# K^T U with 48 stationary columns instead of 64, and its sum into the state in two additions of 48 rows

## The chip, the core and the metric

The kernel runs on one core of a Trainium2 chip. The metric is the device time of one execution in microseconds. The engines of the core are named as in the profile: PE (TensorE, matmuls), PEld (TensorE's loads of the stationary operand, which overlap its matmuls), DVE (VectorE), ACT (ScalarE), POOL (GpSimd) and SP (SyncE, which issues most DMAs).

## What is computed

Two parts follow each other. The first is a delta-rule attention over 4 batches, 8 heads and 768 steps with heads of 48; its result, as 3072 tokens of 384, goes through a two-layer block with an exact GELU (384 to 2048 to 384). Everything is fp32.

```python
# attention: B, H, S, D = 4, 8, 768, 48; k_n is k over its norm
state = zeros(B, H, D, D)
for t in range(S):
    y[:, :, t] = einsum('bhd,bhde->bhe', q[:, :, t], state)
    v_old = einsum('bhde,bhd->bhe', state, k_n[:, :, t])
    state = state + beta_t * einsum('bhd,bhe->bhde', k_n[:, :, t], v_t - v_old)
# second part
x = y.transpose(0, 2, 1, 3).reshape(B * S, H * D)
out = gelu(x @ w_in) @ w_out          # moe_w_in 384 x 2048, moe_w_out 2048 x 384
```

## The kernel before

**Tiling.** The 768 steps are cut into NC = 12 chunks of C = 64 steps. The four batches form two units (a = 0, 1) of two batches each: batch p of a unit lies on partitions 64p to 64p + 63 (HALF[p]), one step per partition, the 8 heads beside each other. A chunk is worked out by matrices instead of step by step: Gram matrices of K (grams), a triangular inverse per head (eliminate_steps on DVE or POOL, then join and join_both through PE), the product of K and Q with the state (against_state, L731; against_queries, L751), the solved update rows U (solve, L791), the outputs (use, L821), and the new state, which is the old one plus K^T U (update, L832, and next_state, L837).

**The state** lies in SQ, a tile of 128 partitions. Its first 48 free elements per head pair are the state (the view St), the 64 after them the transposed Q of the unit. Heads with even number (r = 0) have their 48 state rows on partitions 0 to 47, those with odd number (r = 1) on partitions 64 to 111. Partitions 48 to 63 and 112 to 127 of St are set to zero at the start. Products that read the state or transposed K take rows r\*64 to r\*64 + 47 only.

**K** lies in Kp with 64 elements per head, of which the last 16 are set to zero once (L183) and stay so; the transposes of two heads at a time use that padding.

**K^T U.** For each unit and each chunk but the last, update() issues 16 matmuls: four head pairs j, and the four combinations (r, p) of QUADS. Stationary is K of one head and batch on 64 partitions, moving is U of the same (64 x 48). The result goes to PSUM on the partitions of half r. The PSUM tile psY of two banks holds the outputs (psY) and beside them this sum (psS). The matmuls of one batch and one r use one quarter of the array, so four quarters work side by side.

**After it**, outputs() runs on each unit in turn: next_state() adds psS into the state on DVE (L837), and read() makes the unit's output rows from psY with three DVE instructions (L847; from chunk 2 on): one over all 128 rows and two that swap the halves. When both units are read, turns() (L883; turn(), L873, for chunks 0 and 2) transposes the result on PE, ACT copies it to SBUF as xT, and the two-layer block takes it from there. In chunks 0 and 1 the reads are on ACT (L845), and chunk 0's additions stand after other work on DVE.

**The two-layer block** of chunks 0 and 1 is plain matmuls (fc1 L906, fc2 L924). From chunk 2 on it runs in a form with seven products of halves for eight, with sums made on DVE and ACT: part_of_layer (L1023) for the first layer, second_layer (L957) for the second, mix_x (L988) for sums of xT, mix (L1090 to L1095) for sums of the GELU's result. Its products are chained to each other in order by behind(). The weights arrive with 8 bytes per number and are decoded to fp32 by DVE and ACT up to about 111 us (begin, exponents, mantissas, signed: L251 to L281); each decoded part frees a slot, into which SP fetches the next (L233).

**What sets the order.** Up to chunk 0's additions, all engines run in the order in which the code is written. From there on, a plan gives each step a time in chunks, the steps are written out in the order of these times, and only DVE and POOL run in just that order (manual_schedule, L1429). The order on PE, ACT and SP is chosen by the framework's planner, which places ready instructions by its own estimate of durations, within the dependencies; `together` chains the matmuls of one step to those written before, and `behind` the products of the two-layer block. The waits between engines follow from what the instructions read and write.

Of the kernel before, what the change touches and what calls it, by code (L numbers as in the profile page):

```python
# [14 lines left out]
ALU = mybir.AluOpType  # L15
# [4 lines left out]
def kernel(  # L20
# [28 lines left out]
    nc = tc.nc  # L49
    B, H, S, D = q.shape  # L50
    DM, DF = moe_w_in.shape
    C = 64
# [8 lines left out]
    HALF = [slice(0, C), slice(C, 2 * C)]  # L61
# [10 lines left out]
    def dn(name):  # L72
        return ps.tile([128, 2, 512], F32, tag="dn", name=name)
# [29 lines left out]
    for c in range(NC):  # L103
        for a in range(NA):
            u = tiles[c, a] = Unit()
# [97 lines left out]
    St = SQ[:, :, :, :, 0:D]  # L203
# [602 lines left out]
    def use(us):  # L806

        for u in us:
            if u.c == 0 and u.a == 0:
                u.psY = [ps.tile([128, NP * D], F32, tag="mlp", name="psY").rearrange(  # L810
                    "q (k r d) -> q k r d", r=2, d=D) for s in range(2)]
            else:
                psY = dn("psY")
                both = quarters(psY[:, :, 0:NP * D])
                u.psY = [both[:, s] for s in range(2)]
                u.psS = psY[:, :, NP * D:2 * NP * D].rearrange("q p (j d) -> q p j d", d=D)
            for k in range(NP // 2):
                for r in range(2):
                    for p, s in SIDES:
                        h = 4 * k + 2 * s + r  # L820
                        nc.tensor.matmul(u.psY[s][HALF[p ^ s], k, r, :], lhsT=u.P[HALF[p], h, :],  # L821
                                         rhs=u.U[HALF[p], h, :], start=True, stop=True)
            if u.c > 0:
                update(u)

    def update(u):
        if u.c == 0 and u.a == 0:
            u.psS = dn("psS")[:, :, 0:NP * D].rearrange("q p (j d) -> q p j d", d=D)
        if u.c < NC - 1:
            for j in range(NP):  # L830
                for r, p in QUADS:
                    nc.tensor.matmul(u.psS[HALF[r], p ^ r, j, :], lhsT=u.Kp[HALF[p], 2 * j + r, :],  # L832
                                     rhs=u.U[HALF[p], 2 * j + r, :], start=True, stop=True)

    def next_state(u):
        if u.c < NC - 1:
            nc.vector.tensor_tensor(St[:, u.a], St[:, u.a], u.psS, op=ALU.add)  # L837

    def read(u, copy=nc.scalar.copy):
        u.x = u.U if u.c else wk.tile([128, H, D], F32, tag="y", name="x")  # L840
# [8 lines left out]
    def outputs(us):  # L849
        use(us)  # L850
        for u in us:
            next_state(u)
            read(u)
# [423 lines left out]
    mantissas(2)  # L1277
    turn(first[0])
    update(first[0])
    exponents(1)  # L1280
    turn(first[1])
    update(first[1])
    exponents(2)
    signed(1)
    for u in first[:NA]:
        next_state(u)
# [174 lines left out]
```

## Time and profile before

| | us |
|---|---|
| median of 3 runs | 629.37 (628.44 to 629.87) |
| the profiled execution | 629.47 |
| its span, first to last instruction | 627.7 |
| PE busy in L832, all records | 15.1 |
| DVE busy in L837, 22 instructions | 12.2 |
| mean granted TensorE clock | 0.986 of full speed |

The profile comes from one execution. Its page gives the busy time of each engine, and the busy share in 40 slices of the span (15.7 us each; a 9 is 90% or more). The chain of work that ended last is followed back from the last instruction, at each step to what released it. In the timeline and the groups, a row has the start and the duration in us, the engine, the line of the kernel, the operation, what it writes and reads, the shape and how many instructions are merged in it; in brackets the idle time of the engine before it and what ended that. A row of several merged instructions lasts from the first one's start to the last one's end. An fp32 matmul shows as two loads and two matmul records. Matmul ends are modelled.

The stage up to about 165 us holds the loading and decoding of the weights and chunks 0 to 2 of the attention; from there to 540 us chunks 3 to 11 and the two-layer block of the chunks before run side by side; the rest is the two-layer block of the last two chunks.

### The profile page before, as it was taken

To read this page: it belongs to the slowest core of one execution; us is meant where nothing else is said; L and a number is where in the kernel's file an instruction comes from. 1 tells how busy PE (TensorE), PEld (TensorE's weight loads), DVE (VectorE), ACT (ScalarE), POOL (GpSimd) and SP (SyncE) were. 2 spreads that over 40 slices of the span, in tenths; PEclk is the share of its full clock that TensorE was granted. 3 is DMA by queue.
4 is the path that set the end of the run, shared out by engine and by line. 5 is a ranking of instruction groups with operands and counts; after the bars stand their busy time and mean duration, and the time that the engine had idled before them with its cause. 6 is when DMAs were issued, how large, how long until landed. Compare 5 with 4: busy or idle time off the path is not lost.

```text
span 627.7 us, 19675 instructions
## 1 busy us (share of the span) xinstructions
PE 606.6 (97%) x8358; PEld 541.4 (86%) x8358; DVE 428.5 (68%) x793; ACT 240.6 (38%) x546; POOL 212.8 (34%) x316
## 2 busy tenths in 40 slices
PE   6779999999999999999999999999999999999997
PEld 4667886776899999998899998899998899988997
DVE  6999899999867598564859555859546946422432
ACT  3476876615443255224451134452134222044200
POOL 4045002000379821885222884223884200000000
PEclk9985999999999999999999999999999999999999
DMA  9695766001423452453123533013321001000011
GB/s 135 155 284 145 162 146 180 23 3 38 74 38 47 78 92 35 69 105 39 16 45 54 101 62 38 12 33 62 64 50 18 11 2 28 8 19 1 0 26 26
DMA packets 159575, 39.63 MB, mean 63 GB/s; under 512 B 151168, under 2 KB 154368, under 8 KB 159488
## 3 DMA queue, kind: packets, MB, share of 16 engines
q1 hardware_dynamic: 156816, 37.34, 30.9%
q10 hardware_dynamic: 2672, 1.03, 0.8%
q8 instruction: 66, 1.08, 0.7%
q14 instruction: 21, 0.17, 0.1%
HBM read 33.62 MB, written 4.72 MB: 61 GB/s over the span
## 4 chain that ended last, share of the span: by engine, by line
PE 81%; DVE 10%; DMA 4%; SPq 2%; issue 1%; ACT 1%; DVEq 0%
PE psX L957 13%; PE psY L1023 11%; PE psY L957 9%; PE psX L1023 8%; PE psV L1023 6%; PE psZ L1023 5%; PE psZ L957 4%; PE psV L957 4%; PE psK L731 3%; PE psO L924 3%; PE psG L439 2%; DMA w_raw<-in_moe_w_out_dram 2%; PE psH L906 2%; PE psY L821 2%; PE psU L791 2%; PE psQ L751 2%
## 5 line engine op out<-in xcount | busy, mean ns | idle before, releaser
L376 POOL TENSOR_TENSOR n<-n,half 128x16 f32<-128x16 f32 x10 | 30.9, 3091 | 176.1 <-DVE n L374 118.4
L529 POOL TENSOR_TENSOR Nu<-Nu,tmp 128x30 f32<-128x30 f32 (+14 forms) x120 | 65.7, 548 | 9.4
L527 POOL TENSOR_TENSOR tmp<-Nu 128x30 f32<-128x30 f32 (+14 forms) x120 | 62.5, 521 | 9.4
L1023 PE MATMUL psX<-xT,w_in_sb 128*128 128x256 f32 (+1 forms) x288 | 62.5, 346 | 0.0
L957 PE MATMUL psX<-w_out_sb,G 128*128 128x192 f32 x320 | 56.4, 329 | 0.0
L957 PEld LDWEIGHTS psX<-w_out_sb,G 128*128 128x128 f32 x320 | 52.1, 190 | 0.8
L1023 PEld LDWEIGHTS psX<-xT,w_in_sb 128*128 128x128 f32 x288 | 47.9, 191 | 5.3
L906 PE MATMUL psH<-xT,w_in_sb 128*128 128x256 f32 x192 | 45.8, 395 | 0.7 <-ACT G L912 0.5
L906 PEld LDWEIGHTS psH<-xT,w_in_sb 128*128 128x128 f32 x192 | 37.1, 197 | 8.0 <-ACT G L912 1.4
L924 PE MATMUL psO<-w_out_sb,G 128*128 128x384 f32 x128 | 43.9, 490 | 0.0
L1051 DVE TENSOR_TENSOR psY<-psY,pu 128x512 f32<-128x512 f32 x20 | 14.0, 700 | 40.9 <-PE psY L1023 40.3
L1023 PE MATMUL psY<-xT,w_in_sb 128*128 128x256 f32 (+1 forms) x192 | 41.5, 345 | 0.0
L1006 ACT COPY pu<-psZ 128x512 f32<-128x512 f32 x40 | 23.5, 587 | 38.7 <-PE psZ L1023 36.3
L1006 ACT COPY xT<-psX 128x768 f32<-128x768 f32 x9 | 7.2, 799 | 81.1 <-PE psX L883 81.1
L924 PEld LDWEIGHTS psO<-w_out_sb,G 128*128 128x128 f32 x128 | 23.5, 190 | 14.2 <-issue 0.3
L1023 PEld LDWEIGHTS psY<-xT,w_in_sb 128*128 128x128 f32 x192 | 32.1, 191 | 3.5
L837 DVE TENSOR_TENSOR SQ<-SQ,psY 128x384 f32<-128x384 f32 x21 | 11.6, 552 | 32.5 <-PE psY L832 32.2
L1006 ACT ACTIVATE G<-G 128x512 f32<-128x512 f32 x40 | 25.2, 631 | 19.8 <-DVE G L1059 19.6
L1006 ACT ACTIVATE G<-psY 128x512 f32<-128x512 f32 x20 | 11.9, 596 | 47.4 <-PE psY L1023 47.4
L1059 DVE TENSOR_TENSOR G<-psY,pu 128x512 f32<-128x512 f32 x20 | 13.8, 690 | 22.2 <-PE psY L1023 21.5
L957 PE MATMUL psY<-w_out_sb,G 128*128 128x192 f32 x160 | 28.1, 329 | 0.0
L957 PE MATMUL psZ<-T,pu 128*128 128x192 f32 x160 | 28.1, 329 | 0.0
(204 smaller groups left out, 1374.6 us busy)
## 6 DMA issues: line engine op xcount, KB each, us to landing
Kp<-in_k_dram SPq DMA_DIRECT2D x76, 96.0 KB, 3.2
w_out_sb<-in_moe_w_in_dram SPq DMA_DIRECT2D x24, 256.0 KB, 5.5
w_raw<-in_moe_w_out_dram SPq DMA_DIRECT2D x16, 384.0 KB, 5.2
V<-in_v_dram SPq DMA_DIRECT2D x48, 96.0 KB, 3.1
out_dram<-o_sb SPq DMA_DIRECT2D x40, 96.0 KB, 2.2
Qp<-in_k_dram SPq DMA_DIRECT2D x64, 32.0 KB, 2.3
Qp<-in_q_dram SPq DMA_DIRECT2D x96, 16.0 KB, 2.0
Qp<-in_k_dram SPq DMA_DIRECT2D x64, 16.0 KB, 2.1
```

Source lines behind the costliest of these rows:

```text
L376: nc.gpsimd.tensor_tensor(flat, flat, half, op=ALU.pow)
L439: nc.tensor.matmul(psG[HALF[p], r, i * NP + j, :], lhsT=u.Kt[rows, p, j, :], rhs=(u.Qt if x else u.Kt)[rows, p, j, :], start=True, stop=True)
L527: rows_on.tensor_tensor(tmp, nu[:, j + 1:, j:j + 1].to_broadcast([128, n, j]), nu[:, j:j + 1, 0:j].to_broadcast([128, n, j]), op=ALU.mult)
L529: rows_on.tensor_tensor(nu[:, j + 1:, 0:j], nu[:, j + 1:, 0:j], tmp, op=ALU.add)
L731: nc.tensor.matmul(u.psK[HALF[p], r, j, :], lhsT=u.Kt[rows, p, j, :], rhs=SQ[rows, u.a, p ^ r, j, 0:w], start=True, stop=True)
L906: nc.tensor.matmul(psH, lhsT=w_in_sb[:, f // 2, m, f % 2 * 128:(f % 2 + 1) * 128], rhs=xTs[c][:, m, :], start=(m == 0), stop=(m == NM - 1))
L924: nc.tensor.matmul(u.psO, lhsT=G[:, u.a, f, :], rhs=w_out_sb[:, f, :], start=(f == 0), stop=(f == NF - 1))
L957: nc.tensor.matmul(ps_, lhsT=lhs[:, f, :], rhs=rhs[:, f, :], start=first and f == 0, stop=f == FH - 1, skip_group_check=not first)
L1006: i = fn(*args, **kw)
L1023: nc.tensor.matmul(ps_[:, i], lhsT=lhs[:, f // 2, f % 2 * 128:(f % 2 + 1) * 128], rhs=rhs, start=first and i == 0, stop=True, skip_group_c ...
L1051: nc.vector.tensor_tensor(L1["Y1"], L1["Y1"], L1["pu"][:, 0], op=ALU.add)
L1059: nc.vector.tensor_tensor(half(1, 1), shaped(L1["Y1"]), shaped(L1["pu"][:, 0]), op=ALU.add)
```

## The change

The stationary operand of K^T U loses the 16 zero columns of Kp: 48 columns instead of 64. The result then covers 48 partitions of each half of PSUM instead of 64, and partitions 48 to 63 and 112 to 127 of psS are not written any more. next_state() adds the two pieces of 48 rows (partitions 0 to 47, and 64 to 111) in two DVE instructions instead of one over 128 partitions. The number of matmuls, their moving operand and all else stay as they are.

```diff
             for j in range(NP):
                 for r, p in QUADS:
-                    nc.tensor.matmul(u.psS[HALF[r], p ^ r, j, :], lhsT=u.Kp[HALF[p], 2 * j + r, :],
+                    nc.tensor.matmul(u.psS[r * C:r * C + D, p ^ r, j, :],
+                                     lhsT=u.Kp[HALF[p], 2 * j + r, 0:D],
                                      rhs=u.U[HALF[p], 2 * j + r, :], start=True, stop=True)
 
     def next_state(u):
         if u.c < NC - 1:
-            nc.vector.tensor_tensor(St[:, u.a], St[:, u.a], u.psS, op=ALU.add)
+            for r in range(2):
+                rows = slice(r * C, r * C + D)
+                nc.vector.tensor_tensor(St[rows, u.a], St[rows, u.a], u.psS[rows], op=ALU.add)
```

## The prediction

> **What bounds the kernel now.** I read the page first (busy times, the 40 slices, the chain of work that ended last), then the chain in order of time, then the timeline around every state update, and last the groups of instructions by form. The page:
>
> ```profile
> PE 606.6 (97%) x8358; PEld 541.4 (86%) x8358; DVE 428.5 (68%) x793; ACT 240.6 (38%) x546; POOL 212.8 (34%) x316
> ...
> PE   6779999999999999999999999999999999999997
> ...
> DVE  6999899999867598564859555859546946422432
> ...
> PE 81%; DVE 10%; DMA 4%; SPq 2%; issue 1%; ACT 1%; DVEq 0%
> ```
>
> TensorE (PE) is the bound: 97% busy, 81% of the chain. VectorE (DVE) is below it on average, but in the slices up to about 165 us it is as full as PE, and the 10% of the chain that is DVE lies almost all there: followed in order of time, the chain runs on DVE from 49.6 to 57.6 us, at 61.4, at 64.1 to 66.5, and, with one DMA of 5.4 us between, from 88.2 to 139.0 us. So there are two stages: up to 165 us a microsecond more on DVE is nearly a microsecond more of time; after it, only what makes PE wait counts.
>
> **The change, part 1: weight loads.** update() issues 16 matmuls for each of 22 unit and chunk pairs (11 chunks, two units), 352 in all; L832 has 672 + 32 = 704 records, so each fp32 matmul is two loads and two matmul passes. Their number stays; each load takes 48 columns instead of 64. The views of single groups:
>
> ```profile
> 86.49 0.56 PEld L832 LDWEIGHTS psY<-V,Kp 64*64 64x64 f32 x32
> 86.96 0.56 PEld L821 LDWEIGHTS psY<-V,P 64*64 64x64 f32 x32
> ...
> 259.73 1.02 PEld L751 LDWEIGHTS psQ<-SQ 48*64 48x64 f32 x64 [0.23 <-issue]
> ...
> 166.96 1.02 PEld L439 LDWEIGHTS psG<-Kt 48*64 48x64 f32 x64
> ...
> 335.45 1.55 PEld L731 LDWEIGHTS psK<-SQ,Kt 48*64 48x64 f32 x64 [0.23 <-issue]
> ...
> 62.31 1.09 PEld L577 LDWEIGHTS psJ<-XM,G 32*32 32x32 f32 x64 [0.33 <-DVE w_e L251]
> ```
>
> The reader is to see that an update takes 0.47 us (86.49 to 86.96), and that 64 loads of 64 columns take 1.02 us whether 48 (L751) or 64 (L439) columns stream behind each; only at 112 (L731) do they take 1.55 us. At 48 streamed columns it is thus not the streaming that sets the pace but the 64 loaded columns. No row has 48 loaded columns, so the price is bounded. Best: the update shrinks with the columns, 0.47 x 48/64 = 0.35, 0.12 us saved; streaming would allow it, since 1.55 x 48/112 x 32/64 = 0.33. Worst: nothing, since 64 loads of 32 columns (L577, using two quarters of the array where L832 uses four) still take 1.09 us. I take 0.09, nearer to the best, because L577's missing parallel parts explain why it isn't faster. On the path: the 20 updates of chunks 1 to 10, where PE is the bound; chunk 0's two lie under DVE. **20 x 0.09 = 1.8 us gained (0 to 2.4).**
>
> The Trainium skill ("TensorE: Matmul & The Clock Gate", LDWEIGHTS) makes a load's time proportional to its columns alone, 1/1.2 ns each; with eight loads in each quarter of the array an update would by that save 8 x 13.3 ns = 0.11 us, 20 of them 2.1 us (an estimate). The equal 1.02 us rows agree with it; no row here has 48.
>
> **Part 2: the additions.** next_state() ran one 128-row addition per pair and now runs two of 48 rows, both with 384 elements a row. Rows don't matter to the duration: 64x192 (L847) takes 355 ns on average, 128x192 (L1129) 357. So each half again takes 0.55 us. What follows each instruction matters too:
>
> ```profile
> 265.78 0.55 DVE L837 TENSOR_TENSOR SQ<-SQ,psY 128x384 f32<-128x384 f32 x1 [5.52 <-PE psY L832]
> ...
> 266.25 1.12 DVE L847 TENSOR_TENSOR V<-psY,y 128x192 f32<-128x192 f32 x3
> 266.55 2.57 PEld L957 LDWEIGHTS psY<-w_out_sb,G 128*128 128x128 f32 x16
> ...
> 267.41 0.55 DVE L837 TENSOR_TENSOR SQ<-SQ,psY 128x384 f32<-128x384 f32 x1
> ...
> 267.88 1.12 DVE L847 TENSOR_TENSOR V<-psY,y 128x192 f32<-128x192 f32 x3
> ...
> 269.10 0.74 PEld L883 LDWEIGHTS psX<-ident,V 128*128 128x128 f32 x6
> ```
>
> Between instructions that start at the same row the next one starts 0.08 us before the last has ended (267.41 + 0.55 = 267.96, next at 267.88); where the start row changes, as from the last read (rows 64 up) to the addition (row 0), it starts 0.04 after the end (266.25 + 1.12 = 267.37, next at 267.41). The two halves start at rows 0 and 64, so addition, addition, read costs 2 x 0.585 = 1.17 us where addition, read cost 0.47: **0.70 us more per pair**, 1.40 per chunk.
>
> The Trainium skill says the same of such a pair ("VectorE: DVE Perf Modes", Two Vector instructions with no wait between them): an instruction that starts in another quarter of the partitions than the one before is held until all earlier ones have finished. Without that rule the second addition would cost 0.47 and the sum below would lose a third of its DVE terms.
>
> **Where that lies up to 165 us.** The rows:
>
> ```profile
> 58.58 0.55 DVE L837 TENSOR_TENSOR SQ<-SQ,psS 128x384 f32<-128x384 f32 x1
> 59.05 0.55 DVE L837 TENSOR_TENSOR SQ<-SQ,psY 128x384 f32<-128x384 f32 x1
> 59.51 0.95 DVE L280 SCALAR_TENSOR_TENSOR w_e<-w_out_sb,w_e 128x768 uint32<-128x768 uint32 x1
> ...
> 139.14 1.15 PE L622 MATMUL psJ<-XM,G 32*64 32x64 f32 x32 [0.74 <-DVE XM L538]
> ```
>
> Chunk 0: both additions back to back take 0.93 us to the next start; four halves with a change of row each take 4 x 0.585 = 2.34, so 1.4 late. Queued behind them is the weight decode (L280, L281, L251), which feeds ACT's exponents, the joins at 66.6 and the fc1 matmuls. Chunk 1: the additions start at 87.27 and 88.18, each having waited for PE; now the first pair runs 87.18 to 88.35, the second to 89.52, where the decode went on at 88.65: 0.9 late. DVE is then full until the join at 139.14, so PE gets its matrix 2.3 us late. After it DVE idles 0.88 us (145.06 to 145.95, waiting for PE), which can absorb as much, and is full again to the reads that end at 161.84; chunk 2 adds 1.4: 2.8 late there. The transposes of the second unit (L873, 162.76) come 0.9 after that read: **1.9 us late** for the first layer of chunk 2, which needs both units. Ends: 0.3, if also the 1.6 us from the mixed operand (L988, 164.2) to the first product that reads it (165.86) absorbs; 3.7, if nothing does (1.4 + 0.9 + 1.4). I take 1.9, since those slacks are only there if PE's own work doesn't slide with them. PE's fc2 products (48 records of L924 from 141.9 to 165.2) can fill its waits, but then they are missing later: the first layer's start is what counts.
>
> **After 165 us.** DVE idles 2 to 8 us before each chunk's first addition, so the delay dies out within a chunk; the question is whether PE meets it. The first to need the reads are the transposes in turns() (L883). Chunks 3, 7 and 9 have 5.3 us between the last read and L883 (204.88 to 210.20 in chunk 3), chunk 4 has 2.1: hidden. Chunks 5, 6, 8 and 10 have 0.1 us (reads end at 269.00, 331.82, 425.06, 516.06; L883 at 269.10, 331.94, 425.15, 516.18): a stall of 1.40 - 0.09 - 0.10 + 0.18 = 1.4 us each if PE's order stays (the first shorter update lets DVE start 0.09 earlier; both let PE arrive 0.18 earlier). But PE's order is the planner's, and it can put matmuls of the next product (2.6 us, ready) ahead of the transposes. Then the lateness moves on to the Q transposes on DVE (L429, ending at 334.36) and to L731 at 335.45, 1.1 us behind, where 0.2 to 0.3 is left. So a site costs 0 to 1.4; I take 0.6, a little under the middle, since a wait known to the planner is seldom left whole. **4 x 0.6 = 2.4 us (0 to 5.6).**
>
> No DMA is added or moved; the DMAs that wait for decoded slots (L233) slide with DVE and are in the 1.9.
>
> **Sum:** -1.8 + 1.9 + 2.4 = +2.5 us. The profiled execution took 629.47 us (span 627.7 and 1.8 around it), 0.1 above the median of 629.37: forecast 631.9 us.
>
> **Rivals.**
> A, faster: the planner's order hides the additions. Place: the four turns and the fillers before 165 us; price: 0.3 of the early delay and 0.1 a site, against the loads' full 2.4: 629.4 - 2.4 + 0.3 + 0.4 = 627.7 us. It decides once what is left of the additions falls below the loads' gain. For it: PE's order is free, and ready products lie beside every site. Against: DVE's order is fixed by hand, and up to 165 us it is as full as PE.
> B, order kept: the four stalls are met in full: 629.4 - 1.8 + 1.9 + 5.6 = 635.1. For it: the fit of 0.1 us at four sites shows PE going straight from product to transposes; against: the planner sees the added instructions.
> C, the loads gain nothing: 629.4 + 1.9 + 2.4 = 633.7. For it only L577. Here belongs a rule of the Trainium skill ("TensorEngine Tiling (Array Packing)", Instruction Overhead): a matmul streaming fewer than some 60 columns costs as much as one of 60. That speaks for equal 1.02 us at 48 and 64 columns as well as the loads do, and gives C's time.
>
> **Chances.** Forecast 0.45 (its own range 630.5 to 634.0), A 0.25, B 0.2, C 0.1. A measurement of this kernel tells some 0.2% (1.3 us) from no change: 628.1 to 630.6 is "same". Of A 0.20 is faster and 0.05 same; of the forecast 0.08 and of C 0.02 is same; the rest, with all of B, slower: faster 0.20, same 0.15, slower 0.65. The range takes in A's edge and B: 627.9 to 636.0.
>
> **What would show it.** L832's groups spaced 0.38 us instead of 0.47; 44 additions of 0.55 us in L837, the second of each pair 0.03 after the first, the read 0.03 after that, DVE's busy time up by some 12 us; the wait of L622 (139.14) 2 us later; L883 stalled, or behind matmuls of the next product, in chunks 5, 6, 8 and 10. It is wrong if PE's order is laid differently in places that I can't see from here, if L832's spacing stays at 0.47, or if the join at 139 comes no later.

## The result, and the profile after

The changed kernel took 635.42 us (median of 6 runs, 633.95 to 639.60) against 629.42 us for the kernel before beside it: a ratio of 1.0101, 95% interval 1.0069 to 1.0133, so slower by 4.3 to 8.4 us. A second set gave 634.39 us against 629.55 (ratio 1.0094, 1.0075 to 1.0113). The sign and the range were right; the forecast of 631.9 was too low by some 2.5 to 3.5 us, and the outcome lies at rival B's total (635.1, PE's order kept), which is why it is still inside the range. The profiled execution took 635.08 us with a span of 633.3, 5.6 longer than before. From the additions on its line numbers are 3 higher: L837 is now L840, L847 L850, L873 L876, L883 L886, L957 L960.

First the changed kernel's page: busy times, and the shares of the chain that ended last.

```profile
PE 606.8 (96%) x8358; PEld 539.0 (85%) x8358; DVE 443.1 (70%) x815; ACT 240.4 (38%) x546; POOL 212.4 (34%) x316
...
PE 78%; DVE 13%; ACT 2%; issue 2%; DMA 2%; SPq 1%; DVEq 0%
```

PE's busy time is as before (606.6), and the loads' is 2.4 us less. DVE has 22 instructions and 14.6 us more, and its share of the chain went from 10% to 13% while PE's fell from 81% to 78%: PE does no more work, it waits more. (The prediction expected some 12 us more on DVE, the 22 added durations; by its own 0.70 us a pair it should have been nearer 15, since the additions no longer overlap with what follows.)

**The loads** came out as forecast. The timeline of the changed kernel in chunk 1 (start, duration, engine, line, operation, count):

```profile
88.18 0.46 PEld L832 LDWEIGHTS psY<-V,Kp 64*48 64x48 f32 x32
...
88.54 0.56 PEld L821 LDWEIGHTS psY<-V,P 64*64 64x64 f32 x32
```

From the update's first load to the next group's is 88.54 - 88.18 = 0.36 us, where it was 0.47. In the unrounded records it is 0.360 against 0.467: 0.107 us per update.

**The additions** have the duration forecast, 0.55 us for 48 rows as for 128. The timeline at chunk 0:

```profile
58.20 1.11 DVE L840 TENSOR_TENSOR SQ<-SQ,psS 48x384 f32<-48x384 f32 x2
...
59.35 1.12 DVE L840 TENSOR_TENSOR SQ<-SQ,psY 48x384 f32<-48x384 f32 x2
...
60.50 0.96 DVE L280 SCALAR_TENSOR_TENSOR w_e<-w_out_sb,w_e 128x768 uint32<-128x768 uint32 x1
```

Four additions take 60.50 - 58.20 = 2.30 us to the next start, where two took 0.93: 1.37 us late, and the decode (L280) behind them with it. The join that was at 139.14 is the first of PE's records to show the whole of the delay:

```profile
141.80 0.91 PE L622 MATMUL psJ<-XM,G 32*64 32x64 f32 x24 [1.08 <-DVE XM L538]
```

It comes 2.66 us later. **The turn of chunk 5**, which before ran straight from the product (266.55) to the transposes (269.10):

```profile
268.52 1.12 DVE L840 TENSOR_TENSOR SQ<-SQ,psY 48x384 f32<-48x384 f32 x2 [5.33 <-PE psY L832]
...
269.68 1.13 DVE L850 TENSOR_TENSOR V<-psY,y 128x192 f32<-128x192 f32 x3
...
270.84 1.12 DVE L840 TENSOR_TENSOR SQ<-SQ,psY 48x384 f32<-48x384 f32 x2
...
271.73 0.41 PEld L886 LDWEIGHTS psX<-ident,V 128*128 128x128 f32 x3
...
271.99 1.13 DVE L850 TENSOR_TENSOR V<-psY,y 128x192 f32<-128x192 f32 x3
...
273.17 0.31 PEld L886 LDWEIGHTS psX<-ident,V 128*128 128x128 f32 x3 [1.03 <-DVE V L850]
273.18 0.55 PE L886 MATMUL psX<-ident,V 128*128 128x128 f32 x3 [0.79 <-DVE V L850]
```

PE runs unit 0's three transposes (L886) as soon as it gets there and then stands for 1.03 us, because unit 1's read ends at 271.99 + 1.13 = 273.12. The list of waits has it at all four turns (total, times, longest):

```profile
PEld psX L886 <- DVE V L850: 4.1, 4, 1.0
...
PE psX L886 <- DVE V L850: 3.1, 4, 0.8
```

**Where the time is.** PE's instructions stand in the same order in both kernels except in one place (in chunk 1's turn, at about 91 us, two fc2 matmuls of L927 come behind two of the transposing matmuls of L873, which was L870, instead of ahead of them; matmuls of different quarters that start together are left aside), so its 8358 records can be matched one by one. How much later the same record starts than in the profile of the kernel before:

| kernel | at 165 us | at 600 us | difference |
|---|---|---|---|
| changed | +3.22 | +5.57 | +2.35 |
| changed, second set | +1.95 | +4.24 | +2.29 |

The last column is the same in two executions; the first is not. Up to 165 us DVE also waits for weights on their way in (DMA of w_raw), and these waits differ from one execution to the next (ahead of the same decode instruction, L254 at 106 us, 0.08 us in the kernel before, 0.91 and 0 in the two executions of the changed kernel): two executions that run the same instructions up to 165 us (the kernel before and adds_late below) stand 1.46 us apart there. So what happens after 165 us can be read from one trace, and what happens ahead of it only from medians, or from DVE's own queue.

### The profile page after: what moved, and what is told of

Same layout as the page of the kernel before. It is cut to its first block, busy times and chain, and to the rows that moved or that the text cites. A ratio compares the mean times of both kernels' runs of the same rounds, so it can differ in the third digit from the quotient of the medians.

```text
span 633.3 us, 19694 instructions
## 1 busy us (share of the span) xinstructions
PE 606.8 (96%) x8358; PEld 539.0 (85%) x8358; DVE 443.1 (70%) x815; ACT 240.4 (38%) x546; POOL 212.4 (34%) x316
## 3 DMA queue, kind: packets, MB, share of 16 engines
q10 hardware_dynamic: 2672, 1.03, 0.8%
## 4 chain that ended last, share of the span: by engine, by line
PE 78%; DVE 13%; ACT 2%; issue 2%; DMA 2%; SPq 1%; DVEq 0%
PE psX L960 12%; PE psY L1026 11%; PE psX L1026 8%; PE psY L960 7%; PE psV L1026 6%; PE psZ L1026 5%; PE psV L960 4%; PE psZ L960 4%; PE psG L439 3%; PE psK L731 3%; PE psH L909 3%; DVE SQ L840 2%; PE psT L418 2%; PE psU L791 2%; PE psY L821 2%
## 5 line engine op out<-in xcount | busy, mean ns | idle before, releaser
L960 PE MATMUL psX<-w_out_sb,G 128*128 128x192 f32 x320 | 56.4, 329 | 0.0
L960 PEld LDWEIGHTS psX<-w_out_sb,G 128*128 128x128 f32 x320 | 52.1, 190 | 0.8
L840 DVE TENSOR_TENSOR SQ<-SQ,psY 48x384 f32<-48x384 f32 x42 | 23.2, 552 | 30.7 <-PE psY L832 30.1
L927 PE MATMUL psO<-w_out_sb,G 128*128 128x384 f32 x128 | 44.3, 492 | 0.0
L927 PEld LDWEIGHTS psO<-w_out_sb,G 128*128 128x128 f32 x128 | 23.5, 190 | 14.6 <-DVE w_out_sb L281 0.8
L960 PE MATMUL psY<-w_out_sb,G 128*128 128x192 f32 x160 | 28.1, 329 | 0.0
L960 PE MATMUL psZ<-T,pu 128*128 128x192 f32 x160 | 28.1, 329 | 0.0
```

Of the source, the lines that this page charges most:

```text
L840: nc.vector.tensor_tensor(St[rows, u.a], St[rows, u.a], u.psS[rows], op=ALU.add)
L927: nc.tensor.matmul(u.psO, lhsT=G[:, u.a, f, :], rhs=w_out_sb[:, f, :], start=(f == 0), stop=(f == NF - 1))
L960: nc.tensor.matmul(ps_, lhsT=lhs[:, f, :], rhs=rhs[:, f, :], start=first and f == 0, stop=f == FH - 1, skip_group_check=not first)
```

## The experiments

Theory T going in: each pair of additions makes DVE 0.70 us later; up to 165 us that reaches PE because DVE is the bound there, after it PE meets it in four turns; the loads give back 20 x 0.107. The rivals are named with each run. All ratios are to the kernel before on the same chip in the same call.

### The two halves of the change, each alone

adds_alone: 64 stationary columns, two additions.

```diff
-nc.tensor.matmul(u.psS[r * C:r * C + D, p ^ r, j, :],
-                 lhsT=u.Kp[HALF[p], 2 * j + r, 0:D],
+nc.tensor.matmul(u.psS[HALF[r], p ^ r, j, :],
+                 lhsT=u.Kp[HALF[p], 2 * j + r, :],
```

> Two additions of 48 rows, but 64 stationary columns as before: the additions' price without the loads' gain. Theory T (the additions cost some 3.5 us up to 183 us and 4 turns x 1.0 us after it; the loads give back 20 x 0.107 = 2.1): 629.4 + 3.5 + 4.1 = 637.0 us, 1.6 above the changed kernel; L832's groups 0.47 us apart, L886 waits 1.0 us in chunks 5, 6, 8 and 10. Rival C (the loads gain nothing on the path): the same as the changed kernel, 635.4.

loads_half: 48 columns, and only the first addition. The state's rows 64 to 111 are left out: they stay zero.

```diff
-for r in range(2):
+for r in range(1):
```

> 48 stationary columns and one addition of 48 rows (rows 0 to 47): the state's rows 64 to 111 are left at zero, so DVE has one addition per pair as before and the loads' gain stands alone. Theory T: 20 x 0.107 = 2.1 us less, 627.3. Forecast's term: 627.6. Rival C (no gain on the path): 629.4.

Measured: adds_alone 635.07 us against 629.51 (ratio 1.0090, 1.0074 to 1.0106: 4.7 to 6.7 us slower); loads_half 627.43 (0.9977, 0.9963 to 0.9990: 0.6 to 2.3 us faster). The loads' gain stands on the path and is the size of 20 x 0.107 = 2.1; rival C's 629.4 for loads_half is outside its interval. adds_alone missed: the 7.5 us expected are outside its interval, and it isn't clear of the changed kernel's medians (635.42 and 634.39), so by its median alone rival C's 635.4 would fit too. The expectation had taken T's early part (3.5) from the changed kernel's one trace, with that execution's waits for weights in it. After 165 us its trace has +3.47 us (+2.84 at 165, +6.31 at 600), against +2.35 and +2.29 with 48 columns, and loads_half has -1.71 (-0.66 and -2.37), which is 16 updates x 0.107.

### Early and late

adds_early and adds_late: 64 columns, and the two additions in part of the chunks only.

```diff
-for r in range(2):
-    rows = slice(r * C, r * C + D)
+for rows in ((slice(0, D), slice(C, C + D)) if u.c < 3 else (slice(0, 128),)):
```

with `u.c > 2` in adds_late and `u.c < 2` in adds_c01.

> 64 columns; two additions in chunks 0 to 2 alone, one from chunk 3 on. Theory T: the DVE delay up to 183 us reaches the end whole, 629.4 + 3.5 = 632.9 us, and the wait of L622 that was at 139.14 comes 2.6 later. Rival B as it was predicted (early 1.9, turns 1.4 each): 631.3. Rival P (the delay dies out in later idle time): 630 or less.

> 64 columns; one addition in chunks 0 to 2, two from chunk 3 on. PE's order is that of the kernel before. Theory T: four stalls of 1.0 us at L886 in chunks 5, 6, 8 and 10, nothing elsewhere: 629.4 + 4.1 = 633.5 us. Rival B (1.4 each): 635.0. Forecast's term (0.6 each): 631.8. The early part up to 183 us is as before, within 0.2 us.

> 64 columns; two additions in chunks 0 and 1 alone. Theory T: DVE's queue is 1.36 + 0.92 us later up to the join of chunk 2 and nothing absorbs it, the 0.88 us of DVE idle time behind the join included: 629.5 + 2.3 = 631.8. The prediction's reading (that idle time absorbs 0.88): 630.9.

Measured: adds_early 633.19 us (ratio 1.0049, 1.0031 to 1.0067: +2.0 to +4.2), adds_late 632.36 (1.0050, 1.0033 to 1.0067: +2.1 to +4.2), adds_c01 631.65 against 629.24 (1.0043, 1.0025 to 1.0061: +1.6 to +3.8). The early and the late part are about equal. adds_early excludes rival P (630 or less); its 2.0 to 4.2 holds T's 3.5 and leaves the 1.9 predicted just outside. adds_late excludes rival B's 1.4 per turn (635.0); T's 633.5 and the forecast's 631.8 both lie inside the interval, and the trace decides. PE's order is that of the kernel before, record for record, and chunk 5 reads:

```profile
266.52 1.12 DVE L840 TENSOR_TENSOR SQ<-SQ,psY 48x384 f32<-48x384 f32 x2
...
267.52 0.41 PEld L886 LDWEIGHTS psX<-ident,V 128*128 128x128 f32 x3
267.67 1.13 DVE L850 TENSOR_TENSOR V<-psY,y 128x192 f32<-128x192 f32 x3
...
268.85 0.31 PEld L886 LDWEIGHTS psX<-ident,V 128*128 128x128 f32 x3 [0.92 <-DVE V L850]
268.86 0.55 PE L886 MATMUL psX<-ident,V 128*128 128x128 f32 x3 [0.68 <-DVE V L850]
```

The records behind this wait come later than those ahead of it, and so in chunks 6, 8 and 10; no other step after 165 us is over 0.1 us. From -1.46 at 165 to +2.01 at 600 these are 3.47 us, 0.87 per turn. In the changed kernel a turn costs (2.35 + 1.71)/4 = 1.0: both of the chunk's shorter updates let PE arrive 0.21 us earlier, but only the first lets DVE start earlier, by 0.11.

adds_c01 tells where the early part arises. Its trace stands +2.29 at the join and at 150 us, behind DVE's idle time, and +2.38 at 165 and at 600: a delay that is there at the join stays to the end. The prediction's reading of it (1.4 late) is just outside the interval.

With these sizes the whole change was expected anew:

> The changed kernel once more, beside the three below. Theory T, with sizes from the traces (DVE lateness of chunks 0, 1 and 2 that reaches PE: 1.36 + 0.92 + 0.57; four turns at 1.0; 20 updates at -0.107): 629.5 + 2.85 + 4.0 - 2.1 = 634.2 us. Rival U (something that the traces have not shown, such as the one place in chunk 1 where PE's order differs, adds over a microsecond): 635.4 again.

The second set's 634.39 us is at T's 634.2; its interval (4.7 to 7.1 us slower) holds both, T's 4.7 at its edge, so this run doesn't decide between T and U.

### The order within a pair, and the change of rows

upper_first: the changed kernel with `for r in (1, 0)`.

> As the changed kernel, but of each pair of additions the one of rows 64 up comes first. Theory H (an instruction that starts in another row quarter than the one before starts only after its end; with the same start row 0.08 before it): the second unit's pair then has one change of row instead of three, 0.22 us less to the read; unit 0's pair, chunk 0's and chunk 1's stay. Four turns and chunk 2 less by 0.22: 1.1 us less than the changed kernel of the same call, 633.1. Rival (the price is per instruction, whatever the rows): no difference.

Measured: 632.75 us against 629.55 (ratio 1.0059, 1.0047 to 1.0071); the changed kernel in the same call 634.39. DVE in chunk 5:

```profile
268.87 1.12 DVE L840 TENSOR_TENSOR SQ<-SQ,psY 48x384 f32<-48x384 f32 x2 [5.41 <-PE psY L832]
269.92 1.12 DVE L850 TENSOR_TENSOR V<-psY,y 128x192 f32<-128x192 f32 x3
271.07 1.12 DVE L840 TENSOR_TENSOR SQ<-SQ,psY 48x384 f32<-48x384 f32 x2
272.11 1.11 DVE L850 TENSOR_TENSOR V<-psY,y 128x192 f32<-128x192 f32 x3
```

A pair takes 1.05 us to the read (268.87 to 269.92) instead of 1.16 (268.52 to 269.68 above): the addition next to the read now starts at row 0 as the read does, and the read begins 0.07 before its end. The price per turn falls from 1.0 to 0.76 us ((1.31 + 1.71)/4, with +3.60 at 165 and +4.91 at 600), as theory H has it; a price per instruction alone would have left it. The split was not as expected, though. Each of the two pairs saves 0.11, instead of the second alone 0.22, since the addition at 271.07 still starts 0.03 after the read ahead of it ends (269.92 + 1.12 = 271.04). That read writes rows 64 up but takes its PSUM rows from 0. The Trainium skill ("VectorE: DVE Perf Modes", Two Vector instructions with no wait between them) judges inputs and output apart, and by it this addition, whose inputs start in another quarter than that read's, is held; the trace agrees with its 0.03 us.

### A cheaper way to one addition

mixed: 64 columns for r = 0, so that the rows up to 111 are all written, and one addition of 112 rows.

```diff
+nc.tensor.matmul(u.psS[r * C:C + r * D, p ^ r, j, :],
+                 lhsT=u.Kp[HALF[p], 2 * j + r, 0:(C, D)[r]],
...
+for rows in (slice(0, C + D),):
```

> 64 stationary columns for r = 0 and 48 for r = 1, and one addition of rows 0 to 111. Theory S (loads of the four quarters of the array follow one another, so the group's pace is their mean): L832's groups 0.41 us apart, 20 x 0.054 = 1.1 us less, 628.4. Theory M (the quarters load side by side and the slowest sets the pace): 0.467 as before, 629.5.

Measured: 629.59 us against 629.55 (ratio 1.0009, 0.9999 to 1.0019). Its trace has no step down at the updates: -0.44 at 165, -0.12 at 600, where 16 updates at 0.054 would have taken 0.9. Theory M holds: the quarters of the array take their loads side by side and the widest sets the pace, so narrow loads in two of the four quarters are worth nothing. The single load records show it too. In the kernel before, the loads of the four quarters start within 0.02 us of each other, and each quarter's next one follows 0.058 us later; in the changed kernel it follows 0.045 us later. In mixed, in unit 0's update of chunk 5, the two wide quarters go on every 0.058 us and the two narrow ones, on their own, every 0.045.

### Moving the reads

reads_late2: the changed kernel, but from chunk 2 on both reads first, and the four additions behind.

> As the changed kernel, but from chunk 2 on DVE does both units' reads first and the four additions behind them. Theory T: the four waits of L886 (4.0) and chunk 2's share (0.6) go, what is left is 1.36 + 0.92 - 2.1: 629.6 us. Rival W (the additions, now last, are late for the next matmul that needs the state or for the next tile in the same PSUM buffer, four chunks or more by 1 us): 633 or more. Rival U of the run before: 631.

Measured: 631.98 us (ratio 1.0036, 1.0024 to 1.0049), 2.4 below the changed kernel of the same call where 4.8 were expected; its interval, 631.1 to 632.6, holds none of the three forecasts. The waits for the reads went, but not all of the time:

```profile
267.92 2.26 DVE L850 TENSOR_TENSOR V<-psY,y 128x192 f32<-128x192 f32 x6 [5.36 <-PE psY L832]
...
268.51 2.57 PEld L960 LDWEIGHTS psY<-w_out_sb,G 128*128 128x128 f32 x16
...
270.19 1.70 DVE L840 TENSOR_TENSOR SQ<-SQ,psY 48x384 f32<-48x384 f32 x3
...
271.43 0.20 PEld L886 LDWEIGHTS psX<-ident,V 128*128 128x128 f32 x2 [0.34 <-PE psY L960]
```

The reads end at 267.92 + 2.26 = 270.18, long before PE is at L886, and yet L886 waits 0.34 us. The row names the product on PE, which came last; what fits in time is DVE: the second of the four additions ends some 1.1 us after 270.19, at 271.3, and L886's wait is over at 271.35 by the record of PE's sequencer. Unit 0's additions free the PSUM buffer of psY, and the next tile from that pool is psX. That the four turns lose 0.2 each this way is seen, which is 0.8 of the 2.4 us missing; the rest isn't accounted for; that the buffer is the cause is inferred from the timing, and confirmed only so far as the next run, made from it, loses nothing there.

read_then_add: chunks 0 and 1 as before the change; from chunk 2 on 48 columns, and for each unit its reads and then its two additions.

```diff
-            next_state(u)
-            read(u)
+            for f in (next_state, read) if u.c < 2 else (read, next_state):
+                f(u)
...
+            for rows in (slice(0, 128),) if u.c < 2 else (slice(C, C + D), slice(0, D)):
```

> Chunks 0 and 1 as in the kernel before (64 columns, one addition of 128 rows). From chunk 2 on 48 columns, and for each unit first its reads, then its two additions, rows 64 up first. Theory T: the second unit's read has two additions ahead of it, as before, so the waits of L886 go and the first unit's additions (after which its PSUM buffer is free for L886) are done in time: 629.5 - 18 x 0.107 = 627.6 us; chunk 2's second read up to 0.2 earlier. Rival W (the second unit's additions, now last, hold up what DVE does next): 4 x 0.5 more, 629.5.

> The kernel before with nothing changed but the order from chunk 2 on: each unit's reads ahead of its one addition. Theory T: the turns already had no wait, so only chunk 2's second read, one addition earlier, can gain: 629.5, or up to 0.4 less. If the order by itself were worth something, this run would show it: then 628 or less.

Measured: read_then_add 627.72 us against 629.24 (ratio 0.9973, 0.9960 to 0.9986: 0.9 to 2.5 us faster than the kernel before); read_then_add_64 629.27 (1.0004, 0.9991 to 1.0016), so the order alone is worth nothing and the gain is the loads'. Chunk 5 of read_then_add, and its waits at L886:

```profile
265.75 1.13 DVE L850 TENSOR_TENSOR V<-psY,y 128x192 f32<-128x192 f32 x3 [5.48 <-PE psY L833]
266.91 1.12 DVE L840 TENSOR_TENSOR SQ<-SQ,psY 48x384 f32<-48x384 f32 x2
267.95 1.11 DVE L850 TENSOR_TENSOR V<-psY,y 128x192 f32<-128x192 f32 x3
269.10 1.12 DVE L840 TENSOR_TENSOR SQ<-SQ,psY 48x384 f32<-48x384 f32 x2
```

```profile
L886 PEld LDWEIGHTS psX<-ident,V x54: 139/141/143, 210.4 to 542.4; 128*128 128x128 f32 x54
...
its engine sat idle before it (us, times) until:
who waited for it (us, times):
  ACT xT L1009: 79.1, 9
```

Nothing stands under "sat idle": no turn waits. Unit 1's read has two additions ahead of it, as many as in the kernel before, and unit 1's own two have nothing behind them that is due. After 165 us the trace gains 1.61 us, nearly all of 16 x 0.107 = 1.71. This version beats both kernels.

## Why the prediction was right in sign and short in size

Term by term, in us:

| term | predicted | seen | from |
|---|---|---|---|
| loads | -1.8 | -2.1 | 20 x 0.107, and loads_half |
| chunk 0 at DVE | 1.4 | 1.37 | 58.20 to 60.50 |
| chunk 1 at DVE | 0.9 | 0.92 | from its first addition to the next L280 1.38 us before, 2.30 after |
| idle time behind the join | -0.88 | 0 | next paragraph |
| chunk 2, what reaches PE | 0.5 | 0.57 | adds_early's step at chunk 2's second turn (L876) |
| four turns | 2.4 | 4.0 | 4 x 1.0 |
| sum | +2.5 | +4.8 | |

**Right:** what costs, and where. 0.70 us per pair (1.16 us to the read instead of 0.47), the change of rows as its cause, both places and the four turns, the loads' gain, and the view of DVE as the bound up to 165 us.

**The step that failed first** is "After it DVE idles 0.88 us ..., which can absorb as much". In the changed kernel DVE idles 0.85 us there (it was 0.88):

```profile
148.60 1.74 DVE L634 TENSOR_TENSOR XM<-psJ,gm 32x256 f32<-32x256 f32 x4 [0.85 <-PE psJ L622]
```

In adds_c01 the delay passes it unreduced (+2.29 to +2.38). The idle time is a wait for PE's second group of join matmuls (L622, 144.76). The chain of the kernel before shows what stands ahead of that group:

```profile
139.14 1.15 PE psJ L622 x32
140.29 1.69 PE psK L731 x64
141.99 2.78 PE psO L924 x8
144.76 1.09 PE psJ L622 x64
```

On PE it follows without a pause on the first group, and that one had itself waited for DVE (139.14): so the gap moved with the delay. A gap absorbs lateness only if what ends it doesn't come from the late engine. The prediction named the proviso ("if PE's own work doesn't slide with them") and then took the slack all the same.

**The second** is the size of a turn: "a site costs 0 to 1.4; I take 0.6, ... since a wait known to the planner is seldom left whole". The planner left PE's order at all four turns as it was, and nothing was put into the wait. That would have been rival B with 1.4 per turn, and this was wrong too: the fit is not 0.1 us but 0.5, since L883's first three transposes are unit 0's, and only the fourth needs the read that ended at 269.00; its load starts at 269.48 (the row at 269.10 begins with the first). With what adds_late shows, 1.40 - 0.87 = 0.53 us of each delay is covered. So B's total of 635.1 came about by other parts: early 2.9 instead of 1.9, turns 4.0 instead of 5.6. That the range held owes something to this luck: it reached up to 636.0 for B's sake, and the forecast's own range ended at 634.0, below both medians of the changed kernel.

The two rivals with fewer microseconds fell with the runs: A (the planner hides the additions) because its order didn't move, C (loads gain nothing) by loads_half. The rule of the Trainium skill given with C ("TensorEngine Tiling (Array Packing)", Instruction Overhead) has a matmul of one streamed column take as long as one of 60. C took that to set the pace whatever is loaded, and 0.36 against 0.47 us with the same 48 streamed disagrees with this reading; whether such a floor lies lower, no run here shows. The Trainium skill's rule for weight loads ("TensorE: Matmul & The Clock Gate", LDWEIGHTS) gave 0.11 per update and 2.1 in all, and 0.107 agrees.

**Still open:** the terms sum to +4.8 and the two sets of the changed kernel gave medians of +6.0 and +4.8, with intervals from 4.3 and 4.7 up. If there is more, it lies ahead of 165 us, where two executions of the same instructions stand up to 1.5 us apart. The prediction took DVE as full up to the join at 139.14 and overlooked that in its own trace it waits 0.63 us for weights there (L251, 103.08). The runs can't tell whether a later DVE also makes such waits longer, or what the one changed place of PE's order in chunk 1 is worth.

## What to carry to other kernels

Before counting an idle gap as slack, follow what ends it: if the chain leads back to the engine that will be late, the gap moves along and absorbs nothing. Where two instructions take the place of one on an in-order engine, look first for an order in which the part that someone waits for comes ahead of the part that isn't due: here, with the two chunks where VectorE is the bound left as they were, that turned a loss of 5 to 6 us into a gain of 1.5. And count per consumer: a turn that reads two tiles waits for the second only when it gets to it.

## What the runs showed of the hardware

Loads into the four quarters of the array run side by side, and the widest sets the pace: all 48 columns wide saves 0.107 us of 0.467 per update, 48 columns in two quarters and 64 in the others save nothing (mixed), although the narrow quarters' own loads follow each other faster (every 0.045 us instead of 0.058). Also, whether two VectorE instructions overlap depends on where inputs and output start, each apart: an addition at rows 64 up, right behind a read that wrote rows 64 up out of rows 0 up, started 0.03 us after its end and not 0.07 before it (upper_first). There the inputs alone differ; in the kernel before, an addition at row 0 behind the same read, from which the output alone differs, started 0.04 us after its end (267.37 to 267.41).
